# Clustered attention and a gated FFN on one core: a new kernel with fp16 parts turned by DMA, cluster picks on token rows, exp weights as the stationary operand and the FFN mixed into later attention

## The chip, the cores and the metric

The kernel runs on one core of one Trainium2 chip. The metric is device time in microseconds (us), less is better. A stated time is the median of several executions. The profile is one execution of its own, a few us shorter because it counts from the first to the last instruction (the span). In the profile PE is the matmul engine, PEld its weight loads, DVE the vector engine, ACT the activation engine, POOL the GpSimd engine and SP the engine that issues most DMAs.

## The reference

Four batches of eight heads, 768 tokens, 64 columns a head. Every query and every key belongs to the nearest of 16 centroids of its head, and a query sees only keys of its own centroid. The result goes through a gated FFN.

```
q_assign = argmax(q_n @ c_n, -1); k_assign = argmax(k_n @ c_n, -1)
mask   = q_assign[:, :, :, None] == k_assign[:, :, None, :]
scores = where(mask, q @ k.T / 8, -1e9)
attn   = softmax(scores) @ v                       # 4 x 8 x 768 x 64
x      = attn as (3072 tokens, 512)
out    = (sigmoid(x @ w_gate) * (x @ w_val)) @ w_out   # inner width 1536
```

A query whose centroid has no key gets the plain mean of v. The new kernel keeps that case by adding 1e-30 times the sum of v to every numerator.

## The kernel before

The picks are made with centroids on partitions and tokens along the free axis, so the maximum over centroids is a maximum over partitions. POOL takes it, once for each half of each side of each head, 128 times:

```python
clh = smallp.tile([16, 384], FP)
nc.scalar.copy(clh, cl[r0c : r0c + 16, :])
amh = smallp.tile([16, 384], FP)
nc.gpsimd.partition_all_reduce(amh, clh, 16, bass_isa.ReduceOp.max)
# ... is_equal on DVE (for q also a scaling on ACT) gives 16 more rows of q_aug and k_aug: they make the mask inside the scores
```

In attention v is the stationary operand and the exp weights move, so the normaliser of 384 queries lies on one partition, is inverted there and broadcast:

```python
nc.scalar.activation(es, sc, AF.Exp, bias=nbias)
nc.tensor.matmul(out=av, lhsT=vv[:, j, :], rhs=es, ...)
# ... after six key blocks:
nc.vector.reciprocal(rden, av[64:65, :])
nc.gpsimd.partition_broadcast(rinv, rden)
nc.vector.tensor_tensor(xT[...], av[0:64, :], rinv, ALU.mult)
```

The FFN of all tokens follows after the last head. A scheduler orders the instructions. The weights are loaded first of all.

The softmax here doesn't subtract the row's maximum and nothing guards it: scores larger than these inputs give would overflow.

## Time and profile before

| | us |
|---|---|
| time, median (3 runs, 705.78 to 708.74) | 708.67 |
| span of the profiled run | 702.7 |
| first exp | 72.7 |
| attention, first to last exp | 433 |
| FFN alone | 195 |

From the page of the kernel before: part 1 (busy time and share of the span), two rows of part 2 (tenths busy in 40 equal slices, and the granted PE clock in tenths of full speed), and three groups of part 5 (after the bar: busy us, mean ns of one, then idle time just before them and what ended it).

```profile
PE 541.2 (77%) x1960; PEld 217.8 (31%) x1960; DVE 380.3 (54%) x416; ACT 448.8 (64%) x892; POOL 265.5 (38%) x268
...
PE   0045877676777877677887667977799999999997
...
PEclk9998568897587699569679758575589999999999
...
L209 ACT ACTIVATE es<-sc,nbias 128x384 f16<-128x384 f32 x384 | 206.9, 578 | 29.6 <-PE sc L201 14.6
L177 POOL PARTITION_ALL_REDUCE amh<-clh x128 | 185.0, 1481 | 79.6 <-ACT clh L175 63.1
...
L218 DVE RECIPROCAL rden<-av 1x384 f32<-1x384 f32 x64 | 163.3, 2552 | 23.1 <-PE av L210 21.2
```

The windows table of the kernel before. Columns: stretch and its length, then busy us and instruction count of PE, PEld, DVE, ACT and POOL, the mean granted clock, the DMA share and GB/s.

```profile
0.00:35.00 35.00, 1.49 (x8) 0.92 (x8) 4.58 (x24) 7.10 (x26) 9.58 (x21) 1.00 0.99 151
200.00:350.00 150.00, 112.62 (x360) 42.09 (x360) 111.98 (x110) 125.49 (x253) 95.88 (x92) 0.76 0.21 29
600.00:690.00 90.00, 90.00 (x419) 40.83 (x418) 24.75 (x36) 27.95 (x47) 0.00 (x0) 1.00 0.09 34
```

Three stages with three limits: DMA in the head (share 0.99, PE idle), no single engine in attention (each of PE, DVE, ACT and POOL busy between 64% and 84%, the clock down to 0.76), and PE alone in the FFN (90 of 90 us, 419 matmuls, so 215 ns for 512 columns).

### The profile page before, as it was taken

The page shows a single profiled execution, that of the slowest core. Times are in us where ns is not written, and L with a number is a line of the kernel's source. Part 1 is how long each engine was busy: PE and PEld are TensorE (multiplying, and loading weights), DVE is VectorE, ACT ScalarE, POOL GpSimd, SP SyncE. Part 2 cuts the span into 40 slices and gives each one's busy share as a digit, 9 for nine tenths or more (in the row PEclk, how much of TensorE's full clock was granted, in tenths as well). Part 3 has the DMA queues.
Part 4 walks back from the last instruction along what each step waited for, and adds up shares of the span by engine and source line. Part 5 has one row for each costly group of instructions (what it writes and reads, how often), then busy time and mean ns, then how long its engine had stood idle before and what let it go on. Part 6 is the DMA issues. An engine that isn't in the chain of part 4 may idle for free.

```text
span 702.7 us, 6609 instructions
## 1 busy us (share of the span) xinstructions
PE 541.2 (77%) x1960; PEld 217.8 (31%) x1960; DVE 380.3 (54%) x416; ACT 448.8 (64%) x892; POOL 265.5 (38%) x268
## 2 busy tenths in 40 slices
PE   0045877676777877677887667977799999999997
PEld 0022222332222333222233212222234444444443
DVE  1123578877478777568877648875631313122131
ACT  2168789898787899778899878785532323333232
POOL 3223778524588722588742368661100000000000
PEclk9998568897587699569679758575589999999999
DMA  6993101043300123311023100000001010101101
GB/s 111 191 165 81 44 6 12 7 79 44 80 6 6 12 51 57 73 23 12 6 34 57 23 0 1 0 0 1 0 2 45 16 60 1 61 15 46 44 17 61
DMA packets 81620, 27.21 MB, mean 39 GB/s; under 512 B 75952, under 2 KB 77488, under 8 KB 81584
## 3 DMA queue, kind: packets, MB, share of 16 engines
q1 hardware_dynamic: 53888, 18.91, 10.9%
q0 software_dynamic: 27696, 7.87, 10.9%
q8 instruction: 16, 0.26, 0.2%
q14 instruction: 20, 0.16, 0.1%
HBM read 28.34 MB, written 6.29 MB: 49 GB/s over the span
## 4 chain that ended last, share of the span: by engine, by line
PE 39%; ACT 18%; POOL 16%; issue 14%; DVE 8%; DMA 4%; POOLq 0%; ACTq 0%; DVEq 0%
POOL amh L177 13%; ACT es L209 11%; PE gp L248 9%; PE vp L256 9%; PE op L269 9%; PE av L210 5%; DVE rden L218 4%; DMA vv<-in_v_dram 4%; PE cl L163 4%; PE sc L201 3%; ACT k_aug L152 2%; ACT qkT L154 2%; POOL rinv L220 2%; ACT q_aug L185 1%; DVE k_aug L189 1%
## 5 line engine op out<-in xcount | busy, mean ns | idle before, releaser
L209 ACT ACTIVATE es<-sc,nbias 128x384 f16<-128x384 f32 x384 | 206.9, 578 | 29.6 <-PE sc L201 14.6
L177 POOL PARTITION_ALL_REDUCE amh<-clh x128 | 185.0, 1481 | 79.6 <-ACT clh L175 63.1
L210 PE MATMUL av<-es,vv 128*65 128x384 f16 x384 | 152.1, 402 | 57.6 <-ACT es L209 44.5
L218 DVE RECIPROCAL rden<-av 1x384 f32<-1x384 f32 x64 | 163.3, 2552 | 23.1 <-PE av L210 21.2
L201 PE MATMUL sc<-q_aug,k_aug 80*128 80x384 f16 x384 | 155.1, 409 | 3.3 <-DVE k_aug L189 1.6
L265 DVE TENSOR_TENSOR hT<-g,vp 128x512 f16<-128x512 f32 x72 | 49.5, 687 | 129.0 <-PE vp L256 124.8
L163 PE MATMUL cl<-qkT,cTp 128*64 128x384 f32 x128 | 86.7, 775 | 29.6 <-ACT clh L175 28.4
L264 ACT ACTIVATE g<-gp 128x512 f32<-128x512 f32 x72 | 43.0, 597 | 74.6 <-PE gp L248 74.6
L210 PEld LDWEIGHTS <-vv 128*65 128x65 f16 x384 | 50.7, 134 | 104.6 <-issue 73.3
L220 POOL PARTITION_BROADCAST rinv<-rden x64 | 49.3, 770 | 85.0 <-DVE rden L218 85.0
L175 ACT COPY clh<-cl 16x384 f32<-16x384 f32 x128 | 59.9, 468 | 28.9 <-PE cl L163 19.5
L248 PE MATMUL gp<-xT,wg 128*128 128x512 f16 x288 | 74.8, 382 | 4.1 <-DVE xT L221 4.1
L201 PEld LDWEIGHTS <-k_aug 80*128 80x128 f16 x384 | 42.7, 111 | 109.9 <-issue 98.1
L189 DVE TENSOR_TENSOR k_aug<-clh,amh 16x384 f16<-16x384 f32 x64 | 50.9, 799 | 44.0 <-POOL amh L177 43.3
L256 PE MATMUL vp<-xT,wv 128*128 128x512 f16 x288 | 74.5, 381 | 0.0
L269 PE MATMUL op<-wo,hT 128*128 128x512 f16 x288 | 63.1, 379 | 0.0
L221 DVE TENSOR_TENSOR xT<-av,rinv 64x384 f16<-64x384 f32 x64 | 35.2, 551 | 36.8 <-POOL rinv L220 36.2
L182 DVE TENSOR_TENSOR qoh<-clh,amh 16x384 f16<-16x384 f32 x64 | 43.4, 693 | 17.7 <-POOL amh L177 17.2
L277 ACT COPY osb<-op 128x512 f32<-128x512 f32 x24 | 14.1, 586 | 53.5 <-PE op L269 53.5
L185 ACT ACTIVATE q_aug<-qoh 16x384 f16<-16x384 f16 x64 | 32.8, 519 | 16.1 <-DVE qoh L182 15.2
L248 PEld LDWEIGHTS <-wg 128*128 128x128 f16 x288 | 28.2, 98 | 39.4 <-DVE xT L221 5.3
L256 PEld LDWEIGHTS <-wv 128*128 128x128 f16 x288 | 28.4, 99 | 34.6 <-issue 1.1
(413 smaller groups left out, 304.8 us busy)
## 6 DMA issues: line engine op xcount, KB each, us to landing
qk<-in_q_dram SPq DMA_DIRECT2D x32, 192.0 KB, 2.8
qk<-in_k_dram SPq DMA_DIRECT2D x32, 192.0 KB, 3.1
out_dram<-osb SPq DMA_DIRECT2D x24, 256.0 KB, 2.0
vv<-in_v_dram POOLq DMA_DIRECT2D x32, 96.0 KB, 3.2
wg<-in_moe_w_gate_dram POOLq DMA_DIRECT2D x1, 1536.0 KB, 11.2
wv<-in_moe_w_val_dram POOLq DMA_DIRECT2D x1, 1536.0 KB, 10.7
wo<-in_moe_w_out_dram POOLq DMA_DIRECT2D x1, 1536.0 KB, 17.8
cn<-in_centroids_dram SPq DMA_DIRECT2D x8, 4.0 KB, 5.1
```

Of the source, the lines that this page charges most:

```text
L163: nc.tensor.matmul(out=cl, lhsT=cTp[:, pr, :], rhs=qkT[:, side, cols], start=True, stop=True,)
L175: nc.scalar.copy(clh, cl[r0c : r0c + 16, :])
L177: nc.gpsimd.partition_all_reduce(amh, clh, 16, bass_isa.ReduceOp.max)
L189: nc.vector.tensor_tensor(ka[64:80, cols], clh, amh, ALU.is_equal)
L201: nc.tensor.matmul(out=sc, lhsT=k_aug[:, bass.ts(j, 128)], rhs=q_aug[:, bass.ts(qb, QB)], start=True, stop=True,)
L209: nc.scalar.activation(es, sc, AF.Exp, bias=nbias)
L210: nc.tensor.matmul(out=av, lhsT=vv[:, j, :], rhs=es, start=(j == 0), stop=(j == NCH - 1),)
L218: nc.vector.reciprocal(rden, av[64:65, :])
L220: nc.gpsimd.partition_broadcast(rinv, rden)
L248: nc.tensor.matmul(out=gp, lhsT=wg[:, dcc, fc, :], rhs=xT[:, dcc, bass.ts(t, TB)], start=(dcc == 0), stop=(dcc == NDC - 1),)
L256: nc.tensor.matmul(out=vp, lhsT=wv[:, dcc, fc, :], rhs=xT[:, dcc, bass.ts(t, TB)], start=(dcc == 0), stop=(dcc == NDC - 1),)
L269: nc.tensor.matmul(out=op, lhsT=hT[:, fc, bass.ts(tb, 128)], rhs=wo[:, fc, :], start=(fc == 0), stop=(fc == NFC - 1),)
```

## The change

The intent is to leave PE as the only limit. Tokens go on partitions for the picks, so the maximum is a free-axis reduce. Turning to the other layout is done by DMA transposes of 16-bit data (an fp32 token is split into an fp16 value and an fp16 remainder). The exp weights become the stationary operand, so the normaliser lies beside each query. The FFN of one batch is issued in small pieces between the attention steps of the next, in an order that is written down and not scheduled. It is a new kernel, so the diff is cut to its core; lines between those shown are left out:

```diff
+    ctx.enter_context(tc.manual_schedule())
+    def v_sum(b, p):                       # batches 1 to 3, 12 times
+        POOL.tensor_tensor(s, vr[:, :, 0, :], vr[:, :, 1, :], ALU.add)
+        for c in range(2, NCH):
+            POOL.tensor_tensor(s, s, vr[:, :, c, :], ALU.add)
+        POOL.partition_all_reduce(a..., s..., 128, bass_isa.ReduceOp.add)
+        POOL.memset(sv[:, :, 64:65], TINY * S)
+        POOL.tensor_scalar(sv[:, :, 0:64], a, TINY, None, ALU.mult)
+    def v_sum_pe(b, p):                    # batch 0: the same sum as a matmul with ones
+        ...
+    def prep_split(side, b, h, c0):
+        DVE.tensor_copy(hl[:, c0:, 0:64], r)
+        POOL.tensor_tensor(hl[:, c0:, 64:128], r, hl[:, c0:, 0:64], ALU.subtract)
+        return lambda: SP.dma_start_transpose(out=t[:, c0:, :], in_=hl...)
+    def prep_logits(side, b, h, c0, slot, oh):
+        PE.matmul(out=lg[:, bass.ts(c, 32)], lhsT=t[:, c0 + c, :], rhs=cm[:, h]...)
+        DVE.tensor_reduce(mx[:, 0:n], ls[:, 0:n], AX.X, ALU.max)
+        ...
+    def do_av(s, xT):
+        PE.matmul(out=av[:, c, :], lhsT=s["es"][:, o : o + 128], rhs=VA[b, p][:, e, j, :], ...)
+        DVE.reciprocal(rec[:, 0:nq], t[:, 0:nq, 64:65]...)
+        POOL.tensor_tensor(x, t[:, 0:nq, 0:64], bcast(rec[:, 0:nq], 64), ALU.mult)
+    # in group_tasks: steps of the attention at which the next group is prepared
+        at(s, a)            # split: DVE, POOL
+        at(s + 2, tr)       # transpose: SP, DMA
+        at(s + 9, lgt)      # logits: PE
+        at(s0 + 8 + 20 * i, lambda p=p: v_sum(b, p))
+    # in run_steps, for each attention step
+        do_scores(s)
+        ffn_run(max(0.0, (backlog() - reserve)) / left)
+        do_av(pend.pop(0), xT)
-    # the whole kernel before
```

## The prediction

> **What bounds the kernel now.** Span 702.7 us (time 708.7). The windows table gives three stages. (1) Head: first exp at 72.7 us; in 0 to 35 us the DMA engines are full (0.99), PE is busy 1.5 us: weights, loaded first, share them with q, k, v. (2) Attention, 72.7 to 506 us: no engine is full (200 to 350 us: PE 75%, ACT 84%, DVE 75%, POOL 64%), PE's granted clock 0.71 to 0.76. The chain of waits passes between engines: partition_all_reduce (1.48 us x128), one-partition reciprocal (2.55 us x64), exp (0.58 us x384), fp32 centroid matmuls (0.78 us x128), broadcast. (3) FFN, 506 to 700 us: pure PE, 419 matmuls in 90 us, 215 ns per 512 columns at clock 1.00, weight loads hidden.
>
> **What the change does.**
> - Removes the 128 all-reduces of the max, one-partition reciprocals and broadcasts. With tokens on partitions the max is a free-axis reduce and the reciprocal has 1 to 6 columns.
> - Turns AV: exp is stationary, v (65 columns) moves: 1,152 pairs instead of 384 matmuls of 384 columns (61 us at full clock). The columns cost 27 ns, but each needs a 128x128 load, recorded at 98 ns and no longer hideable. Estimate 65 ns a pair, 75 us.
> - Tanh beside exp replaces sigmoid; exp loses its bias operand. The Trainium skill ("ScalarE: Activation LUTs", What ACT_TABLE_LOAD costs) gives 93 ns per pointer operand: estimate 0.49 us for 352 exps of 384 columns.
> - Turns tokens by DMA: about 84 transposes on the sync queue, 64 hops. The skill ("DMA: Bandwidth & Descriptors") gives 261 GB/s for a hard case: under 1 us of data each. No run here shows it yet; queue issue time is my main doubt.
> - Mixes one batch's FFN into the next one's attention: of the 195 us tail the last batch's stays, 192 x 163 ns + 72 x 215 ns = 47 us.
> - Starts attention before the weights arrive.
>
> **Sum for the new kernel (PE bounds the middle, clock about 1).** A full batch on PE: scores 96 x 163 ns = 16 us, AV 288 x 65 = 19, FFN 47, logits 96 x about 60 = 6: 88 us. ACT per batch about 60 us, DVE 40, POOL 50. Head 45 us (latency chain for batch 0), batch 0: 55, batch 1: 65 (smaller FFN), batches 2 and 3: 88 each, tail 52, imperfect overlap 25, outside the span 6: **425 us**, range **388 to 480**. Chances: faster over 2%: 0.97, within 2%: 0.02, slower: 0.01.
>
> **How much was on the path.** Nearly all of the gain: attention's 433 us of waits become about 320 with three quarters of the FFN inside; about 145 us of FFN tail vanish into it; about 28 us come from the head.
>
> **What would show it right or wrong.** Right: PE over 85% busy in the middle, clock above 0.9; first exp before 35 us; FFN alone for about 50 us at the end; AV pairs at 55 to 75 ns start to start. Wrong: PE waiting for ACT's exp, for transposes (matmuls waiting on DMA; sync queue busy) or for POOL; clock well below 0.9.
>
> **What would make it wrong.** AV pairs at 98 ns add 38 us. DMA transposes issuing slowly (over 2.5 us each fills the in-order sync queue) would stall every batch. A written order without slack stalls PE at each late engine. POOL may slow beside DVE. With perfect overlap and a head of 35 us: about 390.

## More of the kernel before

The instructions of the all-reduce's line in the kernel before (least, median and greatest ns, first and last start):

```profile
L177 POOLq MODIFY_POOL_CONFIG  x2: 11/11/11, 44.2 to 44.3; - x2
...
L177 POOL PARTITION_ALL_REDUCE amh<-clh x128: 1380/1501/1784, 50.0 to 466.5; - x128
```

POOL changed its configuration for the all-reduce once, at 44 us. It then ran 128 all-reduces, with the broadcasts, casts and loads between them, and did not change it again. The first all-reduce starts 5.7 us after the change (its input may have been late as well; nothing there separates the two).

## The result, and the profile after

The new kernel is correct and takes **593.74 us** (591.01 to 594.91, 4 runs) against 707.22 us beside it (704.11 to 708.74). The ratio is 0.8395, interval 0.8353 to 0.8437. It is faster, but by 113 us where 284 had been predicted. The miss is 169 us.

The page after, the rows that answer to those above (POOL's slices added):

```profile
PE 368.4 (62%) x3241; PEld 238.0 (40%) x3241; DVE 167.2 (28%) x498; ACT 241.4 (41%) x568; POOL 152.3 (26%) x254
...
PE   6872364439075553228086572709649399999996
...
POOL 3732134224240333324230332322333201100000
PEclk7765666868687686759688795958959799999999
...
L533 ACT ACTIVATE es<-sc 128x384 f16<-128x384 f32 (+1 forms) x360 | 168.5, 501 | 66.0 <-PE sc L528 48.5
...
L189 POOL PARTITION_ALL_REDUCE vsa<-vs x12 | 13.1, 1095 | 86.4 <-issue 86.4
```

The windows table after:

```profile
200.00:300.00 100.00, 46.49 (x465) 29.17 (x464) 24.28 (x77) 39.37 (x98) 30.61 (x48) 0.70 0.27 60
400.00:531.00 131.00, 107.29 (x964) 64.84 (x965) 40.39 (x103) 78.51 (x184) 26.76 (x40) 0.89 0.23 46
531.00:592.00 61.00, 54.72 (x306) 29.11 (x304) 16.13 (x29) 15.37 (x31) 0.82 (x1) 1.00 0.12 42
```

In the middle no engine is busy half of the time, which is the mark of latency and not of throughput. The waits table after (engine and line that waited, what ended the wait, us in total, times, longest us):

```profile
...
PEld L348 <- DMA Tk<-hl: 124.1, 11, 15.5
PE lg L348 <- DMA Tk<-hl: 122.7, 11, 15.4
POOL xp L224 <- DVE rec L221: 96.0, 20, 13.5
POOL vsa L189 <- issue: 86.4, 12, 10.3
POOL hl L335 <- DVE hl L334: 86.3, 17, 21.3
POOL sv L198 <- issue: 83.5, 12, 7.3
...
PE lg L348 <- DMA Tq<-hl: 66.9, 12, 21.0
```

PE stood 122.7 + 66.9 = 190 us in front of its logits, waiting for transposed tokens. The name that stands there is the DMA. But such a transpose lands 2.8 us after its issue (median), and waits here are up to 21 us long: the transposes were issued late. Two rows further there is a cause for that. POOL stood 86.4 us before its twelve all-reduces and 83.5 us before the twelve instructions that follow them, released by nothing that the profile shows ("issue"). In POOL's timeline after, around one of them (start us, us, instruction, in brackets the idle time before it):

```profile
151.38 1.09 POOL L189 PARTITION_ALL_REDUCE vsa<-vs  x1 [6.02 <-issue]
152.35 0.18 POOL L197 MEMSET sv<- 128x2 f32 x1
159.69 0.57 POOL L198 TENSOR_SCALAR sv<-vsa 128x128 f32<-128x128 f32 x1 [7.16 <-issue]
160.34 0.51 POOL L224 TENSOR_TENSOR xp<-t,rec 128x192 f16<-128x192 f32 x1
160.81 0.91 POOL L335 TENSOR_TENSOR hl<-kraw,hl 128x384 f16<-128x384 f32 x1
```

The all-reduce takes 1.09 us. Before it POOL stands 6 us, after it 7. The subtraction that a transpose needs (the last line) queues behind. What follows from it, from SP's timeline and from PE's in the same stretch:

```profile
161.75 1.21 SPq L338 DMA_TRANSPOSE Tk<-hl  x1
...
164.58 0.34 PE L348 MATMUL lg<-cm,Tk 128*128 128x32 f16 x6 [15.36 <-DMA Tk<-hl]
```

The transpose is issued as soon as the subtraction is done (160.81 + 0.91 us), and lands 2.8 us later, as usual. By then PE has stood 15.36 us. The POOL instructions of lines 189 and 198 after:

```profile
L189 POOLq MODIFY_POOL_CONFIG  x24: 7/11/13, 78.0 to 452.2; - x24
...
L198 POOLq MODIFY_POOL_CONFIG  x24: 98/98/98, 84.8 to 459.1; - x24
```

The kernel before had two such instructions for its 128 all-reduces; this one has 48 for its 12. In the kernel before, all-reduces, broadcasts and casts ran without a change between them, and here the memset after the all-reduce does. The tensor_tensor and tensor_scalar that now surround each all-reduce do not. The Trainium skill names the cost in "GPSIMD Engine Reference", Instruction dispatch: the first call to a freshly loaded kernel (there: a function loaded into POOL) costs about 6 us, "with no visible profile instruction". The trace agrees for the way there (6.02 us above, 7.2 on average) and shows the way back costing as much (7.16 us above, 7.0 on average).

### The profile page after: what moved, and what is told of

Read it like the earlier page. It is cut to its first block, busy times and chain, and to the rows that moved or that the text cites. A ratio compares the mean times of both kernels' runs of the same rounds, so it can differ in the third digit from the quotient of the medians.

```text
span 592.4 us, 8984 instructions
## 1 busy us (share of the span) xinstructions
PE 368.4 (62%) x3241; PEld 238.0 (40%) x3241; DVE 167.2 (28%) x498; ACT 241.4 (41%) x568; POOL 152.3 (26%) x254
## 4 chain that ended last, share of the span: by engine, by line
issue 36%; PE 32%; POOL 17%; DMA 9%; DVE 3%; SPq 1%; ACT 1%; POOLq 0%; DVEq 0%
PE v L410 7%; PE g L395 7%; PE o L427 6%; POOL hl L335 5%; PE sc L528 4%; POOL vs L187 4%; DMA Tk<-hl 3%; POOL vsa L189 2%; PE av L544 2%; POOL xp L224 2%; DMA Tq<-hl 2%; PE lg L254 2%; DMA kraw<-in_k_dram 2%; DMA ohT<-oh 1%; POOL sv L198 1%
## 5 line engine op out<-in xcount | busy, mean ns | idle before, releaser
L533 ACT ACTIVATE es<-sc 128x384 f16<-128x384 f32 (+1 forms) x360 | 168.5, 501 | 66.0 <-PE sc L528 48.5
L544 PEld LDWEIGHTS <-es 128*128 128x128 f16 x1104 | 84.1, 106 | 47.2 <-issue 9.9
L544 PE MATMUL av<-va,es 128*128 128x65 f16 x1104 | 99.6, 204 | 1.9 <-ACT es L533 1.5
L528 PE MATMUL sc<-Tq,Tk 80*128 80x384 f16 x288 | 96.6, 357 | 0.0
L415 DVE SCALAR_TENSOR_TENSOR hT<-th,v 128x384 f16<-128x384 f32 (+2 forms) x108 | 54.9, 509 | 112.3 <-PE av L544 55.9
L348 PE MATMUL lg<-cm,Tk 128*128 128x32 f16 x144 | 7.7, 183 | 122.7 <-DMA Tk<-hl 122.7
L427 PE MATMUL o<-wo,hT 128*128 128x512 f16 x288 | 72.6, 384 | 5.2 <-ACT ob L436 2.7
L395 PE MATMUL g<-xTb,wg 128*128 128x384 f16 x288 | 62.6, 342 | 0.0
L410 PE MATMUL v<-xTb,wv 128*128 128x384 f16 x288 | 61.9, 339 | 0.0
L401 ACT ACTIVATE th<-g 128x384 f32<-128x384 f32 (+2 forms) x108 | 49.3, 457 | 29.8 <-DVE hT L415 16.2
L348 PE MATMUL lg<-cm,Tq 128*128 128x32 f16 x184 | 9.7, 183 | 67.0 <-DMA Tq<-hl 66.9
L528 PE MATMUL sc<-Tq,t 80*128 80x256 f16 (+1 forms) x96 | 30.1, 373 | 9.3 <-DMA Tq<-ohT 9.3
L189 POOL PARTITION_ALL_REDUCE vsa<-vs x12 | 13.1, 1095 | 86.4 <-issue 86.4
```

The source lines that it names most:

```text
L189: POOL.partition_all_reduce(a.rearrange("p h d -> p (h d)"), s.rearrange("p h d -> p (h d)"), 128, bass_isa.ReduceOp.add,)
L395: PE.matmul(out=g[:, 0:n], lhsT=wg[fc // WQ][:, dc, fc % WQ, :], rhs=xT[:, dc, t0 : t0 + n], start=(dc == 0), stop=(dc == NDC - 1),)
L401: ACT.activation(th[:, 0:n], g[:, 0:n], AF.Tanh, scale=0.5)
L410: PE.matmul(out=w[:, 0:n], lhsT=wv[fc // WQ][:, dc, fc % WQ, :], rhs=xT[:, dc, t0 : t0 + n], start=(dc == 0), stop=(dc == NDC - 1),)
L415: DVE.scalar_tensor_tensor(hT[:, fc, 0:n], st[0][:, 0:n], 1.0, w[:, 0:n], ALU.add, ALU.mult)
L427: PE.matmul(out=o, lhsT=hT[:, fc, bass.ts(t, 128)], rhs=wo[fc // 6][:, fc % 6, :], start=(fc == 0), stop=(fc == NFC - 1),)
```

## The experiments

Theory A: POOL stands still about 14 us (6 to 7 going, 7 coming back) around each of the twelve all-reduces; the subtractions, then the transposes, then PE's in-order logits come late. Rival B: DMA transposes and the sync queue are slow in themselves. Rival C: the sums and the all-reduce cost time, not the change of functions. All outputs are right. Each result is the median of the fast ones among four runs, beside runs of the kernel before on the same chip (705.6 to 707.7 us, so times can be compared to about 0.3%). One of e4's four runs, two of e11's and one of e12's counted as slow and are left out.

| run | what | us |
|---|---|---|
| (changed kernel) | | 593.74 |
| e1_sum_on_pe | sums of v on PE | 442.76 |
| e2_two_side_by_side | all-reduces in pairs | 525.08 |
| e3_one_column | all-reduce of 1 column | 585.90 |
| e4_pool_off_path | subtract and multiply on DVE | 436.11 |
| e9_idle_all_reduce | e1 + 12 unread all-reduces | 541.44 |
| e13_idle_adds | e1 + unread adds | 442.95 |
| e14_adds_and_all_reduce | e1 + both | 579.20 |
| e5_loads_spread | e1, bulk loads spread | **412.06** |
| e11_loads_on_act_queue | e1, loads from ACT | 435.16 |
| e12_first_spread | e5, first group spread too | 411.10 |
| e7_w_out_later | e1, w_out later | 445.09 |
| e6_not_mixed | e1, FFN not mixed | 536.91 |
| e8_together | e5 + e7 + DVE | 417.34 |
| e10_spread_and_dve | e5 + DVE | 412.94 |

### e1: the sums on PE

```diff
-            at(s0 + 8 + 20 * i, lambda p=p: v_sum(b, p))
+            at(s0 + 8 + 20 * i, lambda p=p: v_sum_pe(b, p))
```

> Sums of v for batches 1 to 3 on PE (as batch 0 has them), no all-reduce left. Theory A (POOL stands still some 14 us around each of the 12 all-reduces while it changes its loaded functions, and the token subtractions, hence the transposes, hence PE's logits, queue behind): PE's 190 us of waiting at the logits nearly vanish, time 420 to 440 us. Rival B (the DMA transposes and the sync queue are slow by themselves): 560 us or more, logits still waiting over 120 us.

Measured: 442.76 us, 151 us less by one line (ratio to the kernel before 0.6276, interval 0.6239 to 0.6313). In its waits table PE's waits at the logits fall from 190 to 45 us:

```profile
PE lg L348 <- DMA Tq<-hl: 42.2, 13, 10.0
...
PE lg L348 <- DMA Tk<-hl: 2.8, 4, 1.6
```

The time is 3 us above the range that theory A had given, and 45 us of waits are left (e5 takes them up), but most of the loss is gone, as A says. Rival B falls: the transposes and the queue are the same.

### e2: two all-reduces side by side

```diff
-            at(s0 + 8 + 20 * i, lambda p=p: v_sum(b, p))
+        at(s0 + 28, two_sums)    # add, add, all-reduce, all-reduce, scale, scale
```

> Same 12 all-reduces and same sums, but the two of a group stand side by side, so 6 pairs of changes instead of 12. Theory A: about 6 x 14 = 85 us less, near 510 us (490 to 540). Rival B, and rival C (the sums and the all-reduce themselves cost, not the change): 585 to 600 us.

Measured: 525.08 us. With the same sums and the same twelve all-reduces but six changes each way the time falls by 69 us. POOL's idle time around them falls from 170 to 83 us (40.7 + 42.1 in the waits table of e2), and PE's waits at the logits from 190 to 132 us. That is the direction and nearly the size of A (85). C is out as the whole cause. The edit also moves one sum of each pair 20 steps later, which was not tried alone.

### e3: an all-reduce of one column

```diff
+        POOL.memset(a, 0.0)
         POOL.partition_all_reduce(
-            a.rearrange("p h d -> p (h d)"), s.rearrange("p h d -> p (h d)"), 128, ...)
+            a[:, 0, 0:1], s[:, 0, 0:1], 128, ...)
```

> The all-reduce gets 1 column instead of 128 (the fallback sum for queries without keys is then wrong on purpose; it is weighted 1e-30), the changes stay. Theory A: within 2% of the changed kernel, 585 to 600 us, idle stretches of 6 to 7 us before and after each all-reduce as before. Rival C (the work of the all-reduce): well below, toward e1.

Measured: 585.90 us. The all-reduce fell from 1.09 to 0.40 us; twelve times 0.69 is 8.3 us (the added memset takes 12 x 0.20 us back), and the time fell by 7.8. The intervals of the two ratios overlap (0.8255 to 0.8393 here, 0.8353 to 0.8437 for the changed kernel), so this fall is not clear of noise. The idle stretches stayed (83.7 and 85.9 us in all). So its width is a small part at most.

### e4: nothing that PE waits for on POOL

```diff
-        POOL.tensor_tensor(hl[:, c0:, 64:128], r, hl[:, c0:, 0:64], ALU.subtract)
+        DVE.tensor_tensor(hl[:, c0:, 64:128], r, hl[:, c0:, 0:64], ALU.subtract)
-        (eng or POOL).tensor_tensor(x, ..., ALU.mult)
+        (eng or DVE).tensor_tensor(x, ..., ALU.mult)
```

> All 12 all-reduces stay on POOL with their changes, but the token subtractions and the normalising multiplies move from POOL to DVE (some 50 us more on DVE). Theory A: the stalls remain in POOL's row but PE no longer waits for them: 430 to 470 us. Rival B: 560 us or more.

Measured: 436.11 us, with all twelve all-reduces and their changes in place. POOL's timeline of e4 around one of them:

```profile
120.45 1.20 POOL L189 PARTITION_ALL_REDUCE vsa<-vs  x1 [6.14 <-issue]
121.53 0.18 POOL L197 MEMSET sv<- 128x2 f32 x1
128.73 0.67 POOL L198 TENSOR_SCALAR sv<-vsa 128x128 f32<-128x128 f32 x1 [7.03 <-issue]
```

The same 6 and 7 us are there (75.8 + 94.5 us in all), yet the time is no longer than without any all-reduce (e1, 442.76), because the work queued behind them is not what PE waits for next. Moving the work to DVE gains nothing of its own where POOL does not stand still (e10 below, shown there with the loads spread; e1 with the moves alone was not run). So the stall hurts through the order, and not by itself.

### e9, e13, e14: putting the parts back

e9 adds to e1 twelve all-reduces of one column that nobody reads; e13 adds only the five additions of each sum, unread; e14 adds both.

```diff
+        if b > 0:
+            POOL.tensor_tensor(s_, vr[:, :, 0, :], vr[:, :, 1, :], ALU.add)   # e13, e14
+            for c in range(2, NCH):
+                POOL.tensor_tensor(s_, s_, vr[:, :, c, :], ALU.add)           # e13, e14
+            POOL.partition_all_reduce(dum, ident[:, 0:1], 128, ...add)        # e9, e14
```

> e1 (sums on PE, 443 us) plus 12 all-reduces of one column whose result nobody reads, at the places where the changed kernel has its own. Theory A: they bring most of the loss back though nothing waits for them: 560 to 595 us, about 14 us of standing still each. Any theory in which the sums or their consumers matter: 440 to 460 us.

> e1 plus, on POOL, the five adds of each v sum (2.5 us a time, 12 times, unread), no all-reduce. Reading H (POOL has slack when it does not stand still, so its added work is hidden): 440 to 452 us. Reading I (POOL's time is on the path in any case): 465 to 475 us.

> e9 (12 unread one-column all-reduces, 541 us) plus the same five adds before each. If, once POOL stands still 14 us a time, all its further work adds one to one: 541 + 12 x 2.5 = about 571 us (562 to 580). If the adds are hidden here too: 538 to 548 us, and the missing 50 us to the changed kernel's 594 lie elsewhere.

Measured: e9 541.44, e13 442.95, e14 579.20 us. POOL's timeline of e9:

```profile
102.24 0.91 POOL L338 TENSOR_TENSOR hl<-qraw,hl 128x384 f16<-128x384 f32 x1 [0.29 <-DVE hl L337]
108.94 0.40 POOL L209 PARTITION_ALL_REDUCE dum<-ident  x1 [5.78 <-issue]
117.05 0.90 POOL L338 TENSOR_TENSOR hl<-kraw,hl 128x384 f16<-128x384 f32 x1 [7.71 <-issue]
```

e9 fell short of what theory A had said (560 to 595): it brings back 99 of the 151 us. That was the open question for which e13 and e14 were run. The additions alone cost nothing (443 us, hidden in POOL's slack). On top of the unread all-reduces they cost 38 us, somewhat more than their own 30 us (12 x 2.5). Of the last 15 us to 593.74, about 8 may be the all-reduce's width (e3, not clear of noise); the rest, about 7 us, would be the memset and the scaling and was not tried alone. So theory A holds in a sharper form: standing still costs 99 us and also uses up POOL's slack, after which POOL's ordinary work on the sums adds to the time, some 52 us.

### e5, e11, e12: what delays the transposes that are left

In e1 PE still waits 45 us at the logits (the expectation below says 61; I had added shares of the chain of waits, and the waits table is the right number). In the chain of e1 the longest piece of the middle is one transpose:

```profile
96.38 9.61 DMA Tq<-hl
```

It was issued just behind six bulk loads of 384 KB each. e5 issues those three steps apart, e11 issues them together but from another queue, and e12 also splits the first group's loads.

```diff
+        n_load = 0
-                at(s0 - 20, lambda side=side, p=p: load(SP, side, b, p))
+                at(s0 - 20 + 3 * n_load, lambda side=side, p=p: load(SP, side, b, p))   # e5
+                n_load += 1
+                at(s0 - 20, lambda side=side, p=p: load(ACT, side, b, p))               # e11 instead
```

> e1 with one change: the six loads of a group (2.4 MB), issued together, are issued three steps apart. In e1 PE still waits 61 us at the logits, and transposes issued just behind such six loads landed after 7.5 to 9.6 us where the median is 2.8. Theory D (transposes queue behind bulk loads on the same DMA engines): logits waits fall to under 35 us and the time to 415 to 430 us. Rival E (those waits come from POOL's and DVE's order, the loads do not matter): 438 to 448 us.

> e1 with the six loads of a group still together, but issued from the ACT queue, so that transposes of the sync queue do not stand behind them in the same queue. If queue order was what delayed the transposes: 410 to 425 us, as spreading gave. If it was the share of the DMA engines: 435 to 448 us.

> e5 with the first group's six loads in two lots of three (steps 0 and 8 to 12) instead of six at step 0. Theory D once more: the first transposes of batch 1 land sooner, 2 to 7 us less, 404 to 411 us. If the start of attention is held by the transposed pick and its hops instead: 410 to 415 us.

Measured: e5 412.06 us (3 us below the range of theory D), e11 435.16 us, e12 411.10 us. The waits table of e5:

```profile
PE lg L348 <- DMA Tq<-hl: 18.6, 13, 4.2
...
PE lg L348 <- DMA Tk<-hl: 4.6, 3, 2.1
```

Spreading halves the waits (45 to 23 us) and gives 31 us. Another queue gives 8 us (4 if its two slow runs are counted) and leaves 36 us of waits. So standing behind the loads in one queue is the smaller part, and sharing the DMA engines with 2.4 MB at once remains as the larger; it was not tried alone, for e11 also makes ACT issue the loads. The Trainium skill ("DMA: Bandwidth & Descriptors", Issuing engines are not separate DMA queues) says that all queues run on the same 16 engines, and e11 agrees with it: loads from another queue still delay the transposes. e12 shows no difference from e5.

The windows table of e5, which beats both kernels (ratio to the kernel before 0.5861, interval 0.5817 to 0.5904; no other version is clearly faster):

```profile
100.00:200.00 100.00, 80.86 (x904) 54.73 (x905) 44.23 (x148) 68.94 (x177) 34.39 (x48) 0.93 0.61 131
200.00:300.00 100.00, 97.41 (x983) 61.00 (x981) 46.65 (x138) 72.81 (x178) 27.91 (x36) 1.00 0.56 126
347.00:409.00 62.00, 55.33 (x309) 29.35 (x307) 16.16 (x30) 15.99 (x32) 0.83 (x1) 1.00 0.12 42
```

From 200 us to the last exp at 347 us this is the middle that the prediction had described: PE 97% busy and more, the clock at 1.00. From 100 to 200 us PE is still at 81%.

### e7: w_out later

```diff
-            load_wo(0)
-            load_wo(1)              # at the end of the head
+    at(4, lambda: load_wo(0))
+    at(8, lambda: load_wo(1))       # some steps into attention
```

> e1 with the two loads of w_out issued some steps into attention, not at the end of the head. The first transposed pick landed after 8.9 us in the head, with weights moving. Theory D: it lands in under 6 us, the first exp of block 1 comes at about 55 us instead of 61.5, total 433 to 441 us. Rival: head unchanged, 441 to 446 us.

Measured: 445.09 us, no gain. The head did get shorter: the transposed picks landed after at most 6.7 us and block 1's first exp came at 53.2 us and not at 61.5. But the 8 us were given back before the end. Between 60 and 120 us the longest wait at the logits was 10.0 us, as in e1: the first transposes of the next batch still stood behind that batch's loads.

### e6: the FFN not mixed

```diff
-                ffn_run(max(0.0, (backlog() - reserve)) / left)   # in each attention step
+        ffn_two(...); ffn_run(1e9)                                  # after each batch
```

> e1 with the FFN of each batch run alone after that batch's attention. Theory F (mixing hides FFN matmuls under attention that ACT paces at 0.44 us an exp, 42 us a batch): 475 to 515 us, PE idle in attention, ACT above 85% there. Rival G (the mixing gains little, PE's work is the same sum): 440 to 455 us.

Measured: 536.91 us, so mixing is worth 94 us on top of e1, more than expected. F's picture, ACT setting the pace of attention, fits one stretch only: from 200 to 210 us ACT is busy for 9.71 us, but PE for 9.36 us too, with the clock at 0.72. In the five stretches of 10 us after it ACT is busy for 3.35 to 7.38 us and PE for 4.35 to 7.51 us, so something else holds both. PE's waits for the query tiles at the logits rise from 42 to 68 us, probably because attention alone walks through its steps faster and leaves the transposes less time; this reading was not tested, and the parts were not separated.

### e8 and e10: everything together

e8 is e5 with e7's later w_out and e4's two moves to DVE; e10 is e5 with the moves alone.

> Sums on PE, loads spread, w_out later, and the token subtractions and normalising multiplies on DVE. If the waits are separate causes: 405 to 425 us, logits waits under 25 us, PE over 90% busy from 100 us on. If they hide each other: 430 to 440 us.

> e5 (loads spread, 412 us) with the subtractions and normalising multiplies on DVE and w_out loaded as in e5. If moving them helps once the stalls are gone: 400 to 409 us. If POOL was no longer in the way: 409 to 418 us; then e8's 417 us comes from this move, and not from the later w_out, if it is above 414.

Measured: e8 417.34, e10 412.94 us. Moving work off POOL, worth 158 us in e4, is worth nothing once POOL does not stand still. The extra 4 us of e8 come with the later w_out. e8 lies in the range expected for separate causes (405 to 425), but e5 alone is faster, and PE is 79% busy from 100 to 200 us in e8 where over 90% had been expected. Remedies for the same wait do not add up.

## Why the prediction was right or wrong

**The step that failed** is the line "ACT per batch about 60 us, DVE 40, POOL 50", and with it "PE bounds the middle". The v sums' all-reduce was counted as one more POOL operation of about its busy time. Its busy time is indeed small (1.09 us), but each costs a change of POOL's functions there and back: 86.4 + 83.5 = 170 us of standing still over three batches, 57 us a batch, beside 42 us of real work (127 us busy from 61 to 531 us, over three batches). That is 99 us a batch where 50 had been predicted, and more than PE's 88. It also came in lumps of 14 us while PE's order allows nine steps between split and logits, so the overlap failed as well: PE waited for POOL's subtractions, and POOL for reciprocals that DVE takes of PE's results (96.0 us in the waits table), in turn. e1's 151 us are 12.6 us for each of the twelve sums, which held POOL for about 14 us of standing still and 4 us of work. The runs put 151 us of the 169 us miss on this (e1), 99 of them on the unread all-reduces alone (e9). The line "a written order without slack stalls PE at each late engine" stood among the risks. The profile before held the sign: its configuration changed once for 128 all-reduces, among operations that can live with them. The skill's page cited above held the number.

The other 18 us are a balance, by stage: the head 17 more, the tail 9 more, outside the span 5 less, and in the middle 31 more for transposes behind bulk loads (e5) against some 40 less for AV (below). These add up to 12; the last 6 us stay open.

| | predicted us | changed kernel | e5 |
|---|---|---|---|
| until block 1's first exp | 45 | 61.7 | 59.9 |
| middle, to the last exp | 321 | 469 | 288 |
| after the last exp | 52 | 61 | 61 |

- **AV pairs, mis-sized the other way.** I estimated 65 ns a pair from a 98 ns weight load "no longer hideable". PE's timeline after shows three pairs from 505.26 to 505.35 us:

```profile
505.26 0.25 PE L544 MATMUL av<-va,es 128*128 128x65 f16 x3
505.35 0.33 PE L528 MATMUL sc<-Tq,Tk 80*128 80x384 f16 x1
505.52 0.26 PE L544 MATMUL av<-va,es 128*128 128x65 f16 x3
505.61 0.33 PE L528 MATMUL sc<-Tq,Tk 80*128 80x384 f16 x1
```

  That is 30 ns a pair, start to start, at full clock. 1,152 x 35 ns = 40 us of PE that the sum had too much. Taken off the predicted middle (321 - 40 = 281) this comes near what e5 measures (288). That it comes so near is partly luck, for the sum also holds 25 us that I had guessed for imperfect overlap. The recorded durations here are 98 ns for the load and 193 ns for the matmul (medians); what a pair costs in a stream is the distance between starts, 30 ns.
- **The head was too short by 17 us.** Block 1 waits for the picks of batch 0: the transpose of the first pick landed 8.9 us after its issue, and its hops to the key and query tiles 4.6 us after theirs, with the weights moving at the same time. e7 shows that this is real but not worth much alone.
- **Right:** the first exp of all comes at 19.9 us, before the 35 us named. Exp without its bias operand takes 0.49 us (0.494 measured, 0.578 before; the pointer operand costs 93 ns in the Trainium skill, "ScalarE: Activation LUTs", What ACT_TABLE_LOAD costs, against 84 here). The tail is near (61 against 52). The sync queue is not the main limit: a transpose holds it 1.24 us in the median, under the 2.5 us that I had called dangerous. Behind bulk loads it can be more: the transpose issued at 98.94 us in e1 held it 4.31 us. Mixing the FFN works (e6).
- **Clock.** I had said above 0.9. It was 0.70 to 0.79 between 100 and 400 us, where PE had gaps; in e5, with fewer and shorter ones, it was 0.93 and then 1.00. The Trainium skill ("TensorE: Matmul & The Clock Gate", HAM oscillation) names idle gaps above some 3.4 us as what lowers it; the gaps here were up to 21 us. The trace agrees: the matmul after a score matmul starts 0.17 us behind it just before the wait of 15.36 us shown above, 0.27 to 0.30 us behind it in the 4 us after that wait, and 0.16 us from 169.25 us on. So part of the loss from each wait is the slower clock after it. How much in all was not measured.

## What to carry to other kernels

Before trusting a POOL operation's busy time, count the configuration changes around it and the idle time before it and after it: one all-reduce of 1 us among ordinary arithmetic held POOL some 14 us here. When a matmul waits for a DMA, ask first when that DMA was issued and what its input waited for. In a written order a stall matters only through what is queued behind it, so twelve such stalls cost 99 us in one order (e9) and nothing that shows in another (e4). And where small transfers are waited for, try issuing bulk loads in pieces; it gave 31 us here (e5).

## What the Trainium skill lacked or had wrong

- "GPSIMD Engine Reference", Instruction dispatch, has the load of about 6 us on the first call. It lacks that the way back to ordinary operations costs again (83.5 us over 12 times here, 7.0 us each), and which operations live together: 128 all-reduces, 64 broadcasts and their casts ran with one change, while 12 all-reduces among tensor_tensor and tensor_scalar took 12 changes each way.
- "TensorE: Matmul & The Clock Gate", Back-to-back issue gap, gives a sustained 81 ns for pairs with 128 columns and 131 ns with 512. The runs show 215 ns for 512 columns, 162 for 384 (four in 0.65 us), 55 for 128 (four in 0.22 us in e1) and 30 for 65, with a full 128-column fp16 load each. All four fit the formula that the same section gives for a matmul alone at full clock, N / 2.4 + 2.5 ns, which would have given 30 ns for the AV pairs where I guessed 65.
- "DMA: Bandwidth & Descriptors", Latency and other measured facts, gives a transpose's bandwidth. It has no measured time for what decided here: a 128x768 fp16 SBUF transpose holds the issuing queue 1.24 us and lands after 2.8 us in the median, and landed after 9.6 us behind 2.4 MB of loads (e1, at 96.38 us).
